# The second MoE's weights: split in place from a DRAM copy, in both arms of a branch, and large chunks with stationary weights

## The chip, the cores and the metric

The kernel runs on one core of a Trainium2 chip. The core has five engines that each work through their own instructions in order: TensorE (PE; its weight loads are listed as PEld), VectorE (DVE), ScalarE (ACT), GpSimd (POOL) and SyncE (SP), which here only starts DMAs. The metric is the device time of one execution in microseconds.

## What is computed

A linear attention gives x (1152 tokens of 512). A first MoE runs all eight experts on every token and weights them by `P`. A second MoE sends each token to one expert; an expert takes the first `capacity` = 288 of its tokens:

```python
# second MoE, x: 1152 x 512, w1: 8 x 512 x 1024, w2: 8 x 1024 x 512
logits = x @ w_gate
expert_idx = np.argmax(logits, axis=1)
probs = softmax(logits)
gate_w = probs[np.arange(N), expert_idx]
# disp[e, place] = x of the token, for the first 288 tokens of each expert
h = np.maximum(disp[e] @ w1[e], 0.0)
y = h @ w2[e]
out[token] = gate_w[token] * y[place]
```

On this input the experts get 2, 9, 314, 22, 1, 2, 779 and 23 tokens.

## The kernel before

Every fp32 product is made of three: a number is split in `hi` (a cast to the narrower format fp32r, on ACT mostly) and `lo` (the number less hi, a subtraction on DVE or POOL), and hi x hi, hi x lo and lo x hi are summed in PSUM.

Attention and the first MoE come first. Their weights come in units (`r` tiles, loaded by SP at L198 and L200), and a scheduler sets the order of their instructions. The second MoE begins near 910 us, and there each engine takes its instructions in the order of the program (`by_hand`).

The second MoE's weights are 64 pieces of 512 KB, eight an expert: pieces 0 to 3 are w1, 4 to 7 are w2. A piece is loaded raw into a 4 KB slot (`load`, L520, tile `rw`); its hi goes to a second slot (`h`, L558), its lo to a third (`l`, L571). The slots are few, and `take` and `done` hand them round. `Splits` deals the work out in halves of 128x512: hi of piece 4 on DVE, the others on ACT, lo of pieces 0, 3 and 5 on POOL, the others on DVE. `sp.rest(nx)` brings the rest of the next expert's splits, but those of pieces 4, 6 and 7 (`LATE`), which come behind the expert's branch.

The loop over the experts handles the first 64 places of each expert (the small chunk) always: `q1_small` (L1103, L1104: 16 matmuls of 512 columns with the tokens' hi and lo stationary), `gt_small` (a copy from PSUM on ACT, L1109), `ht_small` (L1115, transposes), `relu_small` (hi on ACT, L1122; lo on DVE, L1123, the tile `hhl`), `q2_small` (L1130, L1131, 16 matmuls), `out_small` (y on ACT and DVE, L1138, and a scatter on POOL, L1092). The other 224 places, as chunks of 128 and 96, are handled by `large` in an arm that is taken only where a bit of `mask` says that the expert has more than 64 tokens; here these are experts 2 and 6. Both chunks' rows are loaded ahead for every expert (`rows_load`, L1087). In `large` too the tokens are stationary and the weights move: q1 (L1159 to L1162), transposes of h (L1171), q2 (L1182 to L1184).

```python
            with tc.If(mask & (1 << e)):
                large(e, CHUNKS[1:], tails[e], w1, w2)
        sp.need(nx, range(8))
        sp.done(e)
```

Of the kernel before, what the change touches and what calls it, by code (L numbers as in the profile page):

```python
# [20 lines left out]
def tile_linear_attention_two_moe(  # L21
# [125 lines left out]
    # x and its sums (A11, A21 + A22, .. of the seven products), hi and lo, by group and half of the chunks of a block  # L147
# [10 lines left out]
    # the first group's are in slots: the blocks that are made in pairs, and the single ones  # L158
# [31 lines left out]
    class Unit:  # L190
        """an expert's weights for FQ of its features: chunk 2 i + k of W1 is in half k of the rows"""
# [48 lines left out]
    def a_parts(i, key):  # L240
        """the first keys' first columns come by themselves"""
# [18 lines left out]
    def phi_group(hl, g, d, nm):  # L260
        """x w_phi - max|x w_phi| for one or two tiles of rows, both heads of the pair"""
# [101 lines left out]
    def a_xtrans(i, c):  # L363
# [8 lines left out]
        if len(full) < len(TGS[c]):  # L372
            # of a half tile's block, each head's rows have their own columns
# [23 lines left out]
    def x_sums(g, c):  # L397
        """the seven products' left sides; chunk 2 i + k of x is in half k of the columns"""
# [31 lines left out]
    lgs = {}  # L430
    # of each token: its expert, logits, logits less the largest, expert as a number, slot
# [3 lines left out]
    def gate_logits(g):  # L435
        """x w_gate; of the second half S1 = A21 + A22 by the first rows of w_gate, and A22 by what the others are more"""
# [49 lines left out]
    def zero_fill(what):  # L486
        """empty slots and zero rows, from a part of acc that nothing needs yet"""
# [17 lines left out]
    def take(key, shape, dt, name):  # L505
        """the slot that has been free for the longest"""
        at[key] = free.pop(0)
        return slot_at(at[key], shape, dt, name)

    def load(n, keep):  # L510
        """weights of the second layer's experts, in order: n pieces, but leave the slots for hi of keep's"""
        while n and todo:
            e, i = todo[0]
            if len(free) <= sum(x[0] <= keep and x not in sp.h for x in raws) + (e <= keep) + sp.more:
                break
            del todo[0]
            w, cc, W = (w1b, DC // 4, F) if i < 4 else (w2b, F // P // 4, D)
            raws[e, i] = take(("r", e, i), [P, cc, W], F32, f"rw_{e}_{i}")
            r0 = i % 4 * cc * P
            nc.sync.dma_start(raws[e, i], w[e, r0 : r0 + cc * P, :].rearrange("(c p) f -> p c f", p=P))  # L520
            n -= 1

    class Splits:
# [60 lines left out]
        def rest(self, upto):  # L584
            """all that is left of experts upto and before but the late ones of upto, in the order of the weights"""
            while True:
                left = [(q[0][1:], k) for k, q in self.q.items() if q and q[0][1] <= upto]
                left = [x for x in left if not (x[0][0] == upto and x[1] != "p" and x[0][1] in self.LATE)]
                if not left:
                    break  # L590
# [719 lines left out]
```

## Time and profile before

| | |
|---|---|
| median of 3 runs | 1082.06 us (1081.43 to 1083.75) |
| span of the profiled execution | 1079.5 us (its time as a run isn't listed; the median is 2.6 us above the span) |
| busy: PE, DVE, ACT, POOL | 1037.5, 749.9, 401.6, 526.6 us |
| DMA | 95.21 MB, mean 88 GB/s |
| second MoE, 910 us to the end | 169.5 us |

The table of busy times is a mean over stages: PE is busy for 96% of the span, but its idle time lies nearly all in the second MoE.

### The profile page before, as it was taken

To read this page: it belongs to the slowest core of one execution; us is meant where nothing else is said; L and a number is where in the kernel's file an instruction comes from. 1 tells how busy PE (TensorE), PEld (TensorE's weight loads), DVE (VectorE), ACT (ScalarE), POOL (GpSimd) and SP (SyncE) were. 2 spreads that over 40 slices of the span, in tenths; PEclk is the share of its full clock that TensorE was granted. 3 is DMA by queue.
4 is the path that set the end of the run, shared out by engine and by line. 5 is a ranking of instruction groups with operands and counts; after the bars stand their busy time and mean duration, and the time that the engine had idled before them with its cause. 6 is when DMAs were issued, how large, how long until landed. Compare 5 with 4: busy or idle time off the path is not lost. (4 is left out here: it accounts for less than half of the span.)

```text
span 1079.5 us, 16720 instructions
## 1 busy us (share of the span) xinstructions
PE 1037.5 (96%) x6214; PEld 926.3 (86%) x6214; DVE 749.9 (69%) x1400; ACT 401.6 (37%) x841; POOL 526.6 (49%) x524
## 2 busy tenths in 40 slices
PE   7999999999999999999999999999999998798787
PEld 7999989898899899889988988898899888576566
DVE  6755799996666666666666666666667667946962
ACT  5767543322223222222232232223222235717532
POOL 4656897644454554444455544444542016625631
PEclk9999999999999999999999999999999998989889
DMA  8813132211112111111111111111111433967700
GB/s 272 273 53 89 62 98 79 79 59 40 39 40 59 49 51 39 39 40 39 46 53 59 40 40 40 39 41 59 58 57 63 131 110 104 323 229 239 264 7 25
DMA packets 56024, 95.21 MB, mean 88 GB/s; under 512 B 6206, under 2 KB 25022, under 8 KB 55936
## 3 DMA queue, kind: packets, MB, share of 16 engines
q1 hardware_dynamic: 54544, 91.41, 26.4%
q0 software_dynamic: 1392, 2.63, 0.7%
q8 instruction: 55, 0.90, 0.4%
q14 instruction: 33, 0.27, 0.1%
HBM read 84.25 MB, written 11.51 MB: 89 GB/s over the span
## 5 line engine op out<-in xcount | busy, mean ns | idle before, releaser
L81 POOL TENSOR_TENSOR l<-r,h 128x256 fp32r<-128x256 f32 (+2 forms) x100 | 154.2, 1555 | 351.4 <-ACT h L80 351.4
L681 DVE SCALAR_TENSOR_TENSOR acc<-p,prob,acc 128x512 f32<-128x512 f32 x252 | 188.3, 749 | 105.2 <-PE p L672 105.1
L670 PE MATMUL p<-h,hh 128*128 128x512 f32 x576 | 228.4, 396 | 0.0
L671 PE MATMUL p<-l,hh 128*128 128x512 f32 x576 | 227.4, 395 | 0.0
L672 PE MATMUL p<-h,hl 128*128 128x512 f32 x576 | 227.3, 395 | 0.0
L636 DVE TENSOR_TENSOR ca<-ca,p 128x256 f32<-128x256 f32 (+1 forms) x256 | 112.6, 449 | 70.2 <-PE p L619 68.0
L80 ACT CAST h<-r 128x256 fp32r<-128x256 f32 (+2 forms) x108 | 70.9, 686 | 184.8 <-PE p L672 163.6
L625 ACT ACTIVATE hh<-ca 128x320 fp32r<-128x320 f32 (+1 forms) x128 | 56.2, 442 | 217.9 <-DVE ca L636 217.9
L672 PEld LDWEIGHTS p<-h,hl 128*128 128x128 f32 x576 | 108.4, 188 | 25.6
L670 PEld LDWEIGHTS p<-h,hh 128*128 128x128 f32 x576 | 108.4, 188 | 22.4
L671 PEld LDWEIGHTS p<-l,hh 128*128 128x128 f32 x576 | 108.4, 188 | 22.3
L81 POOL TENSOR_TENSOR lt<-t,ht 128x256 fp32r<-128x256 f32 x144 | 124.9, 896 | 1.3 <-PE pn L349 1.3
L571 DVE TENSOR_TENSOR l<-rw,h 128x512 fp32r<-128x512 f32 x80 | 82.8, 1066 | 15.2 <-ACT h L558 13.3
L571 POOL TENSOR_TENSOR l<-rw,h 128x512 fp32r<-128x512 f32 x48 | 69.7, 1474 | 30.1 <-ACT h L558 23.2
L617 PE MATMUL p<-xh,ht 128*128 128x320 f32 x256 | 79.2, 309 | 0.0
L619 PE MATMUL p<-xh,lt 128*128 128x320 f32 x256 | 79.1, 309 | 0.0
L618 PE MATMUL p<-xl,ht 128*128 128x320 f32 x256 | 79.1, 309 | 0.0
L617 PE MATMUL p<-xs,ht 128*128 128x256 f32 x256 | 72.9, 285 | 0.7 <-DVE cb L636 0.5
L619 PE MATMUL p<-xs,lt 128*128 128x256 f32 x256 | 72.6, 284 | 0.0
L618 PE MATMUL p<-xs,ht 128*128 128x256 f32 x256 | 72.4, 283 | 0.0
L636 DVE TENSOR_TENSOR cb<-cb,p 128x320 f32<-128x320 f32 (+1 forms) x128 | 58.0, 453 | 19.0 <-PE p L619 18.0
L629 DVE SCALAR_TENSOR_TENSOR hl<-ca,hh 128x320 fp32r<-128x320 f32 (+1 forms) x128 | 65.7, 515 | 2.5 <-ACT hh L625 2.0
(253 smaller groups left out, 2296.6 us busy)
## 6 DMA issues: line engine op xcount, KB each, us to landing
r<-w1a SPq DMA_DIRECT2D x36, 512.0 KB, 3.5
r<-w2a SPq DMA_DIRECT2D x36, 512.0 KB, 3.8
rw<-w1b SPq DMA_DIRECT2D x32, 512.0 KB, 6.1
rw<-w2b SPq DMA_DIRECT2D x32, 512.0 KB, 8.4
disp<-acc SPq DMA_DIRECT2D x18, 260.0 KB, 4.9
v<-va SPq DMA_DIRECT2D x8, 325.0 KB, 3.7
rawq<-qT SPq DMA_DIRECT2D x8, 320.0 KB, 4.7
out<-acc SPq DMA_DIRECT2D x9, 256.0 KB, 5.5
```

The costliest lines, as they stand in the source:

```text
L80: nc.scalar.copy(hi, src)
L81: (eng or nc.vector).tensor_tensor(lo, src, hi, ALU.subtract)
L571: en.tensor_tensor(self.l[e, i].rearrange("p c f -> p (c f)")[:, ks], rv, hv, ALU.subtract)
L617: nc.tensor.matmul(ps, ws_[0], xs[0], start=i == 0, stop=False)
L618: nc.tensor.matmul(ps, ws_[0], xs[1], start=False, stop=False)
L619: nc.tensor.matmul(ps, ws_[1], xs[0], start=False, stop=i == DI - 1)
L629: nc.vector.scalar_tensor_tensor(lv[:, qs], src, 0.0, hv[:, qs], ALU.max, ALU.subtract)
L636: nc.vector.tensor_tensor(o, x, ps, ALU.add)
L670: nc.tensor.matmul(ps, a, w.w2[0][:, f, :], start=f == 0, stop=False)
L671: nc.tensor.matmul(ps, a, w.w2[1][:, f, :], start=False, stop=False)
L672: nc.tensor.matmul(ps, b_, w.w2[0][:, f, :], start=False, stop=f == FT - 1)
L681: nc.vector.scalar_tensor_tensor(o, ps, prob[:, t, e : e + 1], o, ALU.mult, ALU.add)
```

## The change

While the first MoE runs, `stage` copies the 64 pieces from the weights to a DRAM tensor `wst`, two at each call, in an order in which a piece is contiguous for each partition. The later loads read `wst`. lo is written over the raw piece (`r.bitcast(R32)`), so a piece needs two slots; hi and lo are whole instructions of 128x1024. All hi are on ACT; expert 0's lo on POOL, all others' on DVE. `aside` puts splits of the next two experts into both arms of the branch, in the taken one between the steps of `large`. `large` handles both chunks at once: for each 128 of the 1024 features, the weights are stationary and 224 tokens move (q1), so that h comes out already transposed, and q2 follows per feature block. Rows of the large chunks are loaded in the taken arm. The PSUM pools become 4 and 4 banks, and the scratch for POOL's DMAs is set to 4096 bytes. Comments are dropped.

```diff
+    def stage(n):
+        for e, i in staged[:n]:
+            src = piece(e, i)
+            nc.sync.dma_start(wst[e, i].rearrange("p (c f) -> p c f", c=src.shape[1]), src)
+        del staged[:n]
...
-            nc.sync.dma_start(raws[e, i], w[e, r0 : r0 + cc * P, :].rearrange("(c p) f -> p c f", p=P))
+            nc.sync.dma_start(raws[e, i], wst[e, i].rearrange("p (c f) -> p c f", c=src.shape[1]))
...
-        HI_V, LO_P, LO_P0, LATE = (4,), (0, 3, 5), (1, 2, 5), (4, 6, 7)
...
+                    le = "v" if e else "p"
+                    self.q["a"].append((e, i))
+                    self.q[le].append((e, i))
...
+            h, l = self.h[n], r.bitcast(R32)
+            self.put(eng, lambda: en.tensor_tensor(l, r, h, ALU.subtract))
...
+        def aside(self, hi, lo):
+            steps = {k: [] for k in "avp"}
+            self.put, put = (lambda eng, f: steps[eng].append(f)), self.put
+            self.run("v", -1, lo)
+            self.run("a", -1, hi)
+            self.put = put
+            return steps
...
                 yield from layer2(*pend)
+                stage(2)
...
+        def q1(f):
+            ps = bank2(1, f"q1_{e}_{c0}_{f}")[:, :w]
+            k, fs = f // 4, slice(f * P, (f + 1) * P)
             for c in range(DC):
+                nc.tensor.matmul(ps, w1[0][c][:, fs], xh[:, c], start=c == 0, stop=False)
+                nc.tensor.matmul(ps, w1[0][c][:, fs], xl[:, c], start=False, stop=False)
+                nc.tensor.matmul(ps, w1[1][c][:, fs], xh[:, c], start=False, stop=c == DC - 1)
+            nc.scalar.activation(hh, ps, AF.Relu)
+            nc.vector.scalar_tensor_tensor(hl, ps, 0.0, hh, ALU.max, ALU.subtract)
+            for k in "av":
+                if aside[k]:
+                    aside[k].pop(0)()
...
+        q1(0)
+        for f in range(F // P):
+            if f + 1 < F // P:
+                q1(f + 1)
+            q2(f)
...
         q = q1_small(e, 0, a, w1)
-        sp.run("a", 2, nx)
+        sp.run("v", 8, (e + 1, AHEAD - 1))
...
         hs.append(relu_small(e, 1, ht))
+        sp.run("a", 8, (e + 1, AHEAD + 1))
...
-        sp.rest(nx)
...
+        aside = sp.aside((e + 2, AHEAD + 1), (e + 2, AHEAD - 1))
...
+            with tc.If(mask & (1 << e)) as more:
+                mine = {k: list(x) for k, x in aside.items()}
+                for chunks in SETS:
+                    large(e, chunks, [rows_load(e, c0, n) for c0, n in chunks], w1, w2, mine)
+                for f in mine["a"] + mine["v"]:
+                    f()
+            with more.Else():
+                for f in aside["a"] + aside["v"]:
+                    f()
...
-    nc = bacc.Bacc("TRN2", target_bir_lowering=False, num_devices=1)
+    nc = bacc.Bacc("TRN2", target_bir_lowering=False, num_devices=1, dynamic_dma_scratch_size=4096)
```

DVE before, behind expert 1's branch (`l_2_4` is lo of expert 2's piece 4; L558 is hi, L571 lo, L1123 the `hhl` of expert 2, L1138 the y of expert 1):

```order
L558 CAST h_2_4_10375<-rw_4_9751 128x512
L571 TENSOR_TENSOR l_2_4_10377<-rw_4_9751,h_2_4_10375 128x512
L558 CAST h_2_4_10375<-rw_4_9751 128x512
L571 TENSOR_TENSOR l_2_4_10377<-rw_4_9751,h_2_4_10375 128x512
L571 TENSOR_TENSOR l_2_6_10383<-rw_6_9755,h_2_6_10381 128x512 x2
L571 TENSOR_TENSOR l_2_7_10388<-rw_7_9757,h_2_7_10386 128x512 x2
L1123 SCALAR_TENSOR_TENSOR hhl_0_10442<-ht_0_10437,hhl_0_10442 128x4x64
L1123 SCALAR_TENSOR_TENSOR hhl_1_10452<-ht_1_10447,hhl_1_10452 128x4x64
L1138 SCALAR_TENSOR_TENSOR y_10455<-q_1_10152,tails_9745,y_10455 64x512
L571 TENSOR_TENSOR l_3_1_10481<-rw_1_10073,h_3_1_10433 128x512 x2
L571 TENSOR_TENSOR l_3_2_10484<-rw_2_10075,h_3_2_10445 128x512 x2
```

DVE now, from the start of expert 1's untaken arm on (L567 is lo, written over `rw`; L1105 the `hhl` of expert 2, L1120 the y of expert 1):

```order
L567 TENSOR_TENSOR rw_4_9808<-rw_4_9808,h_2_4_9886 128x1024
L567 TENSOR_TENSOR rw_5_9810<-rw_5_9810,h_2_5_9887 128x1024
L567 TENSOR_TENSOR rw_6_9812<-rw_6_9812,h_2_6_10242 128x1024
L567 TENSOR_TENSOR rw_7_10162<-rw_7_10162,h_2_7_10243 128x1024
L567 TENSOR_TENSOR rw_0_10164<-rw_0_10164,h_3_0_10244 128x1024
L567 TENSOR_TENSOR rw_1_10166<-rw_1_10166,h_3_1_10245 128x1024
L567 TENSOR_TENSOR rw_2_10168<-rw_2_10168,h_3_2_10246 128x1024
L1210 UNCONDITIONAL_BRANCH
L567 TENSOR_TENSOR rw_3_10499<-rw_3_10499,h_3_3_10524 128x1024
L1105 SCALAR_TENSOR_TENSOR hhl_0_10545<-ht_0_10540,hhl_0_10545 128x4x64
L1105 SCALAR_TENSOR_TENSOR hhl_1_10553<-ht_1_10548,hhl_1_10553 128x4x64
L1120 SCALAR_TENSOR_TENSOR y_10560<-q_1_10225,tails_9803,y_10560 64x512
```

Between two experts' `hhl` stood ten halves of lo and two of hi, of the same expert and the next; now eight whole lo stand there, of the next expert and the one behind it, seven of them in the arm.

ACT before, behind expert 3's branch (L558 is hi, L1109 the copy gt of expert 4, L1122 its relu):

```order
L558 CAST h_4_6_11010<-rw_6_10407 128x1024
L558 CAST h_4_7_11015<-rw_7_10409 128x1024
L558 CAST h_5_0_11049<-rw_0_10700 128x1024
L1109 COPY gt_0_11060<-q_4_0_11040 128x512
L558 CAST h_5_1_11062<-rw_1_10702 128x1024
L1109 COPY gt_1_11064<-q_4_1_11051 128x512
L1122 ACTIVATE hhl_0_11071<-ht_0_11066 128x4x64
L558 CAST h_5_2_11074<-rw_2_10704 128x512
```

ACT now, from the start of expert 3's untaken arm on (L559 is hi, L1091 the copies gt of expert 4; hi of `h_4_4` and `h_4_5` and the y of expert 2 stand ahead of the branch, behind expert 3's relus):

```order
L559 CAST h_4_6_10935<-rw_6_10846 128x1024
L559 CAST h_4_7_10936<-rw_7_10848 128x1024
L559 CAST h_5_0_10937<-rw_0_10850 128x1024
L559 CAST h_5_1_10938<-rw_1_10852 128x1024
L559 CAST h_5_2_10939<-rw_2_10854 128x1024
L1210 UNCONDITIONAL_BRANCH
L559 CAST h_5_3_11217<-rw_3_11192 128x1024
L1091 COPY gt_0_11229<-q_4_0_11208 128x512
L1091 COPY gt_1_11231<-q_4_1_11220 128x512
```

Before, casts also stood between the two gt and behind the first relu; now all eight of an expert's period stand between its relus and the next gt.

SP before, among the loads of the first MoE's units 4 to 7 (`r_4` is unit 4's raw weights):

```order
L198 DMA r_4_1827<-w1a 128x4x256
L198 DMA r_5_1990<-w1a 128x4x256
L200 DMA r_4_1829<-w2a 128x2x512
L198 DMA r_6_2130<-w1a 128x4x256
L200 DMA r_5_1992<-w2a 128x2x512
```

and now at the same place (L523 is a copy into `wst`):

```order
L198 DMA r_4_1830<-w1a 128x4x256
L523 DMA wst<-w1b 16x8192
L523 DMA wst<-w2b 256x1x512
L198 DMA r_5_1995<-w1a 128x4x256
L523 DMA wst<-w2b 256x1x512 x3
L523 DMA wst<-w1b 16x8192
L200 DMA r_4_1832<-w2a 128x2x512
L523 DMA wst<-w1b 16x8192 x2
L198 DMA r_6_2137<-w1a 128x4x256
```

About four copies stand between one unit's loads and the next's; all 64 come before the loads of unit 12.

## Rows read from the trace of the kernel before

**Rows 1.** Windows of the second MoE: busy us (instructions) of each engine, clock, DMA.

```profile
930.00:950.00 20.00, 13.87 (x58) 10.74 (x59) 19.42 (x21) 11.30 (x15) 12.82 (x10) 0.79 1.04 346
...
990.00:1010.00 20.00, 12.94 (x53) 10.32 (x53) 19.23 (x18) 11.38 (x15) 14.29 (x11) 0.83 0.81 265
```

**Rows 2.** Waits of PE from 905 us on: total, times, longest.

```profile
PE q L1130 <- DVE hhl L1123: 21.9, 6, 5.4
```

**Rows 3.** Timeline of PE: the first instruction of experts 1 to 6, large arms too.

```profile
921.15 0.47 PE L1103 MATMUL q<-h,xhl 128*128 128x512 f32 x1
...
934.14 0.47 PE L1103 MATMUL q<-h,xhl 128*128 128x512 f32 x1 [0.30 <-PEq L1245]
...
952.51 0.93 PE L1146 MATMUL xst<-ident,xs 128*128 128x128 f32 x8
...
977.77 0.39 PE L1103 MATMUL q<-h,xhl 128*128 128x512 f32 x1
978.00 0.40 PE L1104 MATMUL q<-l,xhl 128*128 128x512 f32 x1
...
988.63 0.47 PE L1103 MATMUL q<-h,xhl 128*128 128x512 f32 x1 [0.30 <-PEq L1245]
...
1007.96 0.47 PE L1103 MATMUL q<-h,xhl 128*128 128x512 f32 x1
...
1022.79 0.47 PE L1103 MATMUL q<-h,xhl 128*128 128x512 f32 x1 [0.30 <-PEq L1245]
...
1038.91 0.93 PE L1146 MATMUL xst<-ident,xs 128*128 128x128 f32 x8
```

**Rows 4.** Timeline of PE: q2's first matmuls after a gap, and matmuls behind one.

```profile
929.82 0.50 PE L1130 MATMUL q<-h,hhl 128*128 128x512 f32 x1 [2.55 <-DVE hhl L1123]
...
945.99 0.79 PE L1130 MATMUL q<-h,hhl 128*128 128x512 f32 x1 [5.45 <-DVE hhl L1123]
...
947.43 0.63 PE L1131 MATMUL q<-l,hhl 128*128 128x512 f32 x1
947.86 0.63 PE L1130 MATMUL q<-h,hhl 128*128 128x512 f32 x1
```

**Rows 5.** Timeline of DVE: lo of a whole slot, and of halves.

```profile
174.07 1.21 DVE L81 TENSOR_TENSOR l<-r,h 128x1024 fp32r<-128x1024 f32 x1
...
939.05 1.65 DVE L571 TENSOR_TENSOR l<-rw,h 128x512 fp32r<-128x512 f32 x1
...
971.19 0.69 DVE L571 TENSOR_TENSOR l<-rw,h 128x512 fp32r<-128x512 f32 x1
```

**Rows 6.** DVE's groups by shape from 905 us on: busy us, mean ns, idle before.

```profile
L571 DVE TENSOR_TENSOR l<-rw,h 128x512 fp32r<-128x512 f32 x76 | 80.1, 1087 | 15.2 <-ACT h L558 13.3
L558 DVE CAST h<-rw 128x512 fp32r<-128x512 f32 x14 | 14.3, 1019 | 1.1 <-DVEq L1245 0.9 <-DMA rw<-w1b 0.2
L1123 DVE SCALAR_TENSOR_TENSOR hhl<-ht,hhl 128x256 fp32r<-128x256 f32 x16 | 6.2, 417 | 3.5 <-ACT hhl L1122 3.5
L1138 DVE SCALAR_TENSOR_TENSOR y<-q,tails,y 64x512 f32<-64x512 f32 x8 | 5.9, 736 | 3.1 <-ACT y L1137 2.8 <-ACTq L1245 0.3
```

**Rows 7.** ACT's groups by shape from 905 us on.

```profile
L558 ACT CAST h<-rw 128x1024 fp32r<-128x1024 f32 x40 | 40.4, 1045 | 11.0 <-issue 6.1 <-POOL l L571 2.3 <-PEq L1245 2.0
L1109 ACT COPY gt<-q 128x512 f32<-128x512 f32 x16 | 9.4, 584 | 9.3 <-PE q L1104 7.1 <-DVEq L1245 1.2 <-DVE h L558 1.1
```

**Rows 8.** Timeline of PE in attention: matmuls of 256 columns.

```profile
20.23 0.28 PE L272 MATMUL pjq<-wbd_h,hlkq 128*128 128x256 f32 x1
20.35 0.22 PE L270 MATMUL pjq<-wbd_h,hhkq 128*128 128x128 f32 x1
```

**Rows 9.** Window of the first MoE: busy us, clock, DMA share, GB/s.

```profile
100.00:150.00 50.00, 49.09 (x369) 44.61 (x368) 38.23 (x70) 27.14 (x70) 44.07 (x49) 1.00 0.27 85
```

**Rows 10.** DMA issues at 124 to 129 us and at 990 to 1010 us: median us to landing.

```profile
r<-w1a SPq DMA_DIRECT2D x1, 512.0 KB, 3.4
...
xs<-disp SPq DMA_DIRECT2D x1, 195.0 KB, 9.0
```

More of the change, by code (lines that the diff above doesn't have):

```diff
@@ L508, in take, with piece @@
         return slot_at(at[key], shape, dt, name)
+    staged = [(e, i) for e in range(E) for i in range(8)]
+    wst = dram.tile([E, 8, P, 4 * P * DC // 2], F32, name="wst")
+    def piece(e, i):
+        w, cc = (w1b, DC // 4) if i < 4 else (w2b, F // P // 4)
+        r0 = i % 4 * cc * P
+        return w[e, r0 : r0 + cc * P, :].rearrange("(c p) f -> p c f", p=P)
+    def stage(n):
[3 more added lines that the diff above has]
+        del staged[:n]
     def load(n, keep):
@@ L513, in load @@
             e, i = todo[0]
-            if len(free) <= sum(x[0] <= keep and x not in sp.h for x in raws) + (e <= keep) + sp.more:
+            if len(free) <= sum(x[0] <= keep and x not in sp.h for x in raws) + (e <= keep):
                 break
             del todo[0]
-            w, cc, W = (w1b, DC // 4, F) if i < 4 else (w2b, F // P // 4, D)
-            raws[e, i] = take(("r", e, i), [P, cc, W], F32, f"rw_{e}_{i}")
-            r0 = i % 4 * cc * P
-            nc.sync.dma_start(raws[e, i], w[e, r0 : r0 + cc * P, :].rearrange("(c p) f -> p c f", p=P))
+            src = piece(e, i)
@@ L533, in __init__ @@
+            self.put = lambda eng, f: f()
             for e in range(E):
                 for i in range(8):
[L535 to L540 removed]
@@ L576, in done @@
         def done(self, e):
-            free.extend(at[k, e, i] for k in "hl" for i in range(8))
+            free.extend(at[k, e, i] for k in "hr" for i in range(8))
         def run(self, eng, n, upto):
-            while n and self.q[eng] and self.q[eng][0][1] <= upto:
-                n -= self.emit(eng, n)
[L584 to L590, printed above, removed]
-                self.emit(min(left)[1])
+            while n and self.q[eng] and self.q[eng][0] <= upto and self.q[eng][0] in raws:
+                self.emit(eng)
+                n -= 1
@@ L822, in moe1_run @@
                         old = [at_ring((w, nx)[j].k, m) for j, m in LAST]
-                        free.extend(old[:12])
+                        free.extend([f"f{n}" for n in range(3)] + old[:12])
                         load(8, -1)
+                        sp.run("p", 6, (0, 7))
                 pend = (u, g, w, h)
@@ L835, in moe1_run @@
         h = yield from layer1(u, 0, w)
-        sp.need(0, range(2))
         free.extend(f"x{n}" for n in range(7))
-        load(7, -1)
+        sp.run("p", 8, (0, 7))
+        load(8, 1)
         yield from layer2(*pend)
@@ L913, in moe1_run @@
         C.turn(2, 2)
+        sp.run("a", 5, (1, 7))
         C.logits(1)
@@ L1062, in tile_linear_attention_two_moe @@
     rings["d"] = ctx.enter_context(pool("ring3", reuse_waits="tile"))
-    free.extend([f"d{n}" for n in range(8)] + ["e0"])
+    free.extend([f"d{n}" for n in range(8)] + ["e0", "e1"])
     tails0 = yp.tile([P, E, RW - D], F32, name="tails0")
@@ L1244, in tile_linear_attention_two_moe @@
                 mask = nc.values_load(many[0:1, 0:1], min_val=0, max_val=(1 << E) - 1)
-            with tc.If(mask & (1 << e)):
-                large(e, CHUNKS[1:], tails[e], w1, w2)
-        sp.need(nx, range(8))
+            with tc.If(mask & (1 << e)) as more:
[7 more added lines that the diff above has]
+                    f()
+        load(8, E)
         sp.done(e)
-        load(4, e + 2)
-        if e + 2 < E:
-            tails[e + 2] = [rows_load(e + 2, c0, n) for c0, n in CHUNKS[1:]]
-        load(8, e + 2)
+        load(4, E)
     out_small(E - 1, done)
```

183 lines of the change are left out of this document (55 added, 128 removed).

## The prediction

> **What bounds the kernel now.** I read the windows of 20 us first, then PE's waits, then PE's row of starts, then DVE and ACT by operation. Up to about 890 us (attention and the first MoE) TensorE is never short of work, and the change gives it nothing there; so the place to look is the last 170 us, the second MoE. There PE is busy 13.9 and 12.9 of 20 us in the two windows shown, while DVE is busy 19.4 and 19.2 [rows 1]. The list of waits names the culprit: q2's first matmul waits 21.9 us in all, six times, for `hhl` of L1123, a DVE instruction [rows 2]. The starts of the experts on PE give the price [rows 3]. Experts 3 and 7 follow the two taken large arms and are quick (977.77 to 988.63: 10.9 us, which is about what PE needs for a small chunk). Five others are gated: expert 1 from 921.15 to 934.14 (13.0), expert 2 to 952.51 (18.4), expert 4 from 988.63 to 1007.96 (19.3), expert 5 to 1022.79 (14.8), expert 6 to 1038.91 (16.1): **81.6 us**. The large arm takes 25.3 us (952.51 to 977.77), and comes twice. After a gap of 2.55 us q2 goes on at once, after one of 5.45 us its matmuls start 0.43 us apart [rows 4] instead of 0.23 (977.77 to 978.00 [rows 3]): the clock has fallen to its lower level, and the gap is paid a second time.
>
> Why is `hhl` late? DVE works in order, and ahead of it stand the weight splits of this expert's pieces 4, 6, 7 and, one expert earlier, 1 and 2: ten halves of lo and two halves of hi for each expert. A half of lo takes 0.69 us when POOL is quiet (971.19) and 1.65 us when POOL splits too (939.05) [rows 5]; the means are 1.087 and 1.019 us [rows 6]. With two hhl (0.417) and one y (0.736), DVE needs 10 x 1.087 + 2 x 1.019 + 2 x 0.417 + 0.736 = **14.5 us** for an expert. That is the gated period.
>
> **The change, part by part.** *DVE alone.* Now it takes all eight lo, whole: 1.21 us for 128x1024 at 174.07 us, where POOL didn't work beside it [rows 5]. POOL's part is gone after expert 0, DVE's casts too: 8 x 1.21 + 0.834 + 0.736 = **11.3 us** an expert, and 0.3 as a mean for xhl, which comes every second expert.
>
> *ACT alone for hi.* Eight casts of 1.045, two gt of 0.584 [rows 7], two relus and one y (for these I take DVE's 0.417 and 0.736 for the same tiles): 11.1 us, and ACT can't cast while it waits for q1 or ht. The order puts all eight casts between the relus of one expert and gt of the next, so gt waits for them: some 8.4 us, of which q2 and the next q1 on PE cover about 8. This loop of about 11 us with 1 to 2 us of handing over is the one that I expect to set the period, with DVE close behind.
>
> *Loads.* Eight pieces of 0.52 MB are 4.2 MB an expert. At the 346 GB/s of the window 930 to 950 [rows 1] that is 12.1 us. This would be the bound if each expert had to be fetched in its own period. It has not: 41 pieces are left for the loop, 41 x 1.5 = 62 us of the 135 us that it lasts, and the large arms, when DMA has nothing else, take their share. A piece now needs two slots instead of up to three, so loads go further ahead.
>
> So a gated period is at best 11.3 (DVE or ACT without any handing over) and at worst as now. I walked the three queues through expert by expert with these durations and got 12.9, 12.2, 14.9, 11.9 and 13.8 for experts 1, 2, 4, 5 and 6: **65.7 us, or 15.9 less**. (Five times 11.3 would be 56.5, a gain of 25.1; nothing gained would be 81.6.) Experts 0, 3 and 7 I leave as they are.
>
> *Both arms split.* In the taken arm one cast and one lo stand behind each relu and `hl`. Per f, ACT then has 0.4 + 1.05 and DVE 0.4 + 1.21, against PE's 2.5 us or more: hidden. If a cast in the arm waited for its load, relu behind it on ACT, and with it PE, would wait too; the order shows only pieces there that were asked for a whole expert earlier.
>
> *The large arm.* Per arm: eight transposes as now, 0.93; 96 matmuls of 224 columns; 48 of 512 columns at 0.23 = 11.2. 256 columns start 0.12 us apart (20.23 and 20.35 [rows 8]); by columns 224 are 0.105, and 0.12 is the upper end, so I take 0.113: 10.8 us. The sixteen transposes of h fall away. To the 22.9 come about 1.1 for the first x split and for the last f, whose relu and `hl` nothing covers: **24.0 instead of 25.3, 2.5 less for both** (2.5 is the value for 0.113; 0.12 makes it 1.1, 0.105 makes it 4).
>
> *Rows in the arm.* Two loads now start only when SP has reached the branch. SP gets there an expert early, when it isn't held by a slot: I take nothing. If it comes as late as PE, the price is at most a load behind others, 9.0 us for such rows [rows 10], in each arm.
>
> *The copies.* 64 DRAM to DRAM copies stand on SP's queue among the first twelve units' r loads. No such copy is in the trace. Bounds: a piece's 1.5 us at 346 GB/s, or twice that, since it is read and written: 97 to 194 us of DMA. The stretch of some 190 us in which they run has its DMA engines busy for 0.27 [rows 9], so 139 us are free. An r load landed 3.4 us after its issue [rows 10] and POOL then has its sums to make before PE needs the unit, so a copy or two ahead of it is no loss: I take nothing, with the upper end (194 - 139 = 55 us of DMA work too many, some of which the later units absorb) kept for the rival.
>
> *Scratch of 4096.* It could make the scatters on POOL follow each other more slowly. Nothing that the first two experts need hangs on the last of them, and of the outputs only the last scatter matters: nothing.
>
> **Sum** against the profiled span: 1079.5 - 15.9 - 2.5 + 1.5 (one gap of about 3 us will still bring the clock down for part of a q2: half of 16 matmuls, 0.2 us more each) = 1062.6. The median of the runs is 2.6 above the span, and I leave that: **1065 us**, 17 less.
>
> **A rule against it.** The new large loop cycles through two PSUM banks, q1 to relu to `hl` to q2, where the old one had matmuls in runs of 24. In the trace, gaps up to 2.55 us cost no clock [rows 4], and the new loop's waits should be under 0.5 us, so by the rows the arm stays at the upper level. The Trainium skill, "TensorE: Matmul & The Clock Gate" (A second HAM failure mode: psum-queue depth-cycling), says that short idle times between groups of matmuls which cycle through PSUM banks can be enough to make the clock swing between its levels. By that rule the arm would lose instead of gain; it is rival 3, priced there from rows.
>
> **The rivals.** 1. *Less gain* (22%). ACT's eight casts in a row hold gt, DVE waits for them, and each gated period stays at about 15 us: 75 instead of 81.6, with the arms 1082.06 - 6.6 - 2.5 = 1073. For it: DVE's lo already waits 13.3 us for ACT's casts [rows 6], and ACT gets the 14 half casts that DVE does now. Against it: of DVE's 14.5 us, 3 are gone.
> 2. *More gain* (8%). Everything is ready, and the gated experts come at 10.9 as expert 3 does: 54.5, a gain of 27.1, with the arms 1052.
> 3. *The clock falls in the large arm* (6%), the slower side. Its 22 us of matmuls would take 0.43/0.23 as long: 41, 19 more in each arm, 38 for both: 1103. It decides (17 us) as soon as the lower level holds for 45% of the arms. Against it: no wait there that I can find is longer than 0.5 us.
> 4. *Copies hold up the first MoE* (5%), slower too. With 2.4 us and more for a copy, r loads come later than POOL's slack allows, and PE, never idle there now, waits: 17 to 40 us more, so 1083 to 1105.
> 5. *No change* (5%). The loads bound each expert at 12.1 and a wait for a slot comes on top, so the periods stay: 1082.
>
> **How the numbers follow.** The first case, my forecast, has 54%, and its own range is 1058 to 1070 (terms of 1 to 4 us for each of two arms, and 2 us for a period or two). The range of 1054 to 1078 takes in all of that, nearly all of rival 1 and some of rival 2, about 8 in 10. About 0.2% (2 us) is what a measurement of this kernel can tell from no change. Faster: my forecast and rivals 1 and 2, 84%. Same: 5%. Slower: 11%.
>
> **What would show it.** In the new profile, DVE's lo should be near 1.2 us, with no POOL split beside it after expert 0. PE's wait for `hhl` should fall from 21.9 to under 12 us, and what is left may be put down to gt (ACT). The large arm should take 23 to 25 us at full clock, with 224 columns at 0.105 to 0.12. PE should stay fully busy between 100 and 250 us, and unit starts there move by under 1 us. I am wrong if DMA landings, not DVE or ACT, end the waits of q1 and q2; if the clock in the large arm shows its lower level; or if the span up to 890 us grows.

## The result and the profile after

The changed kernel takes **1056.6 us** (median of 4 runs, 1053.85 to 1059.04) where the one before, run beside it, takes 1081.74: a ratio of 0.9767, 95% interval 0.9736 to 0.9798, or 25 us less. The profiled execution has a span of 1055.9 us (1057.68 as a run), against 1079.5.

The stretch that the prediction was read from comes first. These are the windows of 20 us of the changed kernel (busy us of PE, PEld, DVE, ACT, POOL with their instructions, granted clock, DMA share, GB/s), the same stretch as in [rows 1]:

```profile
930.00:950.00 20.00, 17.67 (x99) 14.75 (x98) 11.91 (x16) 10.84 (x18) 7.95 (x2) 0.91 0.99 368
950.00:970.00 20.00, 20.00 (x123) 17.04 (x121) 9.07 (x12) 7.68 (x13) 1.92 (x2) 1.00 0.08 26
970.00:990.00 20.00, 16.09 (x78) 12.96 (x77) 15.31 (x18) 17.51 (x24) 11.86 (x2) 0.91 0.91 351
990.00:1010.00 20.00, 16.82 (x88) 13.24 (x86) 17.57 (x18) 15.76 (x22) 15.79 (x2) 0.97 0.67 250
```

PE is now the busiest engine in two of the four, at 17.67 and 20.00 of 20 us; DVE, which filled the windows before with over 19, is at 9 to 18, and the clock stands at 0.91 and more instead of 0.79 and 0.83. The large arm (most of 950 to 970) runs at the full clock with hardly a load. What PE still waits for in the second MoE (total, times, longest; compare [rows 2]):

```profile
PE q L1112 <- DVE hhl L1105: 5.3, 3, 1.8
PE ht L1097 <- ACT gt L1091: 3.8, 3, 1.7
```

`hhl` is down from 21.9 to 5.3 us, and beside it the wait for `gt`, a copy on ACT, has grown from 0.3 us to 3.8. And these are PE's starts of the experts from 0 to 7, large arms too (those lines that begin with an xst transpose), the counterpart of [rows 3]:

```profile
907.54 0.47 PE L1085 MATMUL q<-h,xhl 128*128 128x512 f32 x1
...
917.41 0.47 PE L1085 MATMUL q<-h,xhl 128*128 128x512 f32 x1
...
929.03 0.47 PE L1085 MATMUL q<-h,xhl 128*128 128x512 f32 x1 [0.30 <-PEq L1210]
...
941.99 0.38 PE L1132 MATMUL xst<-ident,xs 128*128 128x128 f32 x2
...
965.70 0.39 PE L1085 MATMUL q<-h,xhl 128*128 128x512 f32 x1
...
976.01 0.47 PE L1085 MATMUL q<-h,xhl 128*128 128x512 f32 x1 [0.30 <-DVE y L1120]
...
990.89 0.47 PE L1085 MATMUL q<-h,xhl 128*128 128x512 f32 x1
...
1001.29 0.47 PE L1085 MATMUL q<-h,xhl 128*128 128x512 f32 x1 [0.30 <-DVE y L1120]
...
1016.82 0.38 PE L1132 MATMUL xst<-ident,xs 128*128 128x128 f32 x2
...
1040.53 0.39 PE L1085 MATMUL q<-h,xhl 128*128 128x512 f32 x1
```

Differences of such starts give the ledger (in the kernel before, expert 0 starts at 910.67 us and expert 7 at 1064.11). "Gated five" are the small chunks of experts 1, 2, 4, 5 and 6. "Routing" is the time from the start of the first MoE's last matmul to that of the loop's first; in it the tokens are dealt out to their experts:

| us | before | after | less |
|---|---|---|---|
| gated five | 13.0 + 18.4 + 19.3 + 14.8 + 16.1 = 81.6 | 11.6 + 13.0 + 14.9 + 10.4 + 15.5 = 65.4 | 16.2 |
| routing | 16.7 | 10.0 | 6.8 |
| two large arms | 25.3 + 25.2 | 23.7 + 23.7 | 3.0 |
| experts 0, 3, 7 and the tail | 36.7 | 35.5 | 1.2 |
| up to the first MoE's last matmul | 893.9 | 897.6 | -3.6 |
| span | 1079.5 | 1055.9 | 23.6 |

Two lines of it I had not forecast: the 6.8 us of the routing, and the 3.6 us that the part before it lost.

**The routing.** First the kernel before: the last matmuls of the first MoE end at 894.3 us; then PE has to wait for a one-hot row `oh` on DVE (L735). DVE, POOL and PE there:

```profile
892.73 3.23 DVE L735 TENSOR_TENSOR oh<-iota_e,rt_e 128x16 bf16<-128x16 f32 x1
...
892.42 0.97 POOL L785 DMA_INDIRECT disp<-acc,slot_i  x1 [0.31 <-issue]
893.40 2.51 POOL L571 TENSOR_TENSOR l<-rw,h 128x512 fp32r<-128x512 f32 x2
...
896.01 0.17 PE L750 MATMUL cp<-oh,tri_b 128*128 128x8 bf16 x1 [1.69 <-DVE oh L735]
```

A comparison of 16 numbers a partition lasts 3.23 us, until POOL's two splits are through (893.40 + 2.51 = 895.91). PE stands still for 1.69 and soon after 0.9 us, and then the clock drops: the next window has PE busy all the time at a granted clock of 0.50, the lower level.

```profile
900.00:905.00 5.00, 5.00 (x24) 5.00 (x25) 2.50 (x14) 4.33 (x6) 3.90 (x4) 0.50 0.12 41
```

In the changed kernel POOL has no splits there. The same instruction, and a window of its routing stretch (897.6 to 907.5):

```profile
896.35 0.18 DVE L727 TENSOR_TENSOR oh<-iota_e,rt_e 128x16 bf16<-128x16 f32 x1
```

```profile
898.00:903.00 5.00, 5.00 (x52) 4.99 (x51) 4.10 (x25) 3.46 (x6) 0.86 (x1) 1.00 0.64 188
```

It takes 0.18 us, PE doesn't wait for it, and the clock is full. (The two windows don't hold the same instructions, so their counts don't compare; the 16.7 and 10.0 us of the whole stretch do.) A scatter of POOL ran beside this `oh` too (896.06 us, 0.97), so it is the split, not the scatter, that held it. By the Trainium skill, "SBUF — State Buffer" (SBUF: two separate sides), a DVE instruction with two SBUF inputs and a POOL instruction that reads SBUF exclude each other for a whole instruction. The end of `oh` agrees with that: it comes at 895.96 us, just behind the splits' 895.91. Its start doesn't settle it: as the trace has it, `oh` starts 0.67 us ahead of the splits.

### The profile page after: what moved, and what is told of

It reads as the page before. It is cut to its first block, busy times and chain, and to the rows that moved or that the text cites. A ratio compares the mean times of both kernels' runs of the same rounds, so it can differ in the third digit from the quotient of the medians.

```text
span 1055.9 us, 16779 instructions
## 1 busy us (share of the span) xinstructions
PE 1028.5 (97%) x6278; PEld 923.9 (87%) x6278; DVE 721.9 (68%) x1370; ACT 404.2 (38%) x840; POOL 509.8 (48%) x484
## 5 line engine op out<-in xcount | busy, mean ns | idle before, releaser
L621 DVE SCALAR_TENSOR_TENSOR hl<-ca,hh 128x320 fp32r<-128x320 f32 (+1 forms) x128 | 69.5, 544 | 2.3 <-ACT hh L617 1.6
L628 DVE TENSOR_TENSOR cb<-cb,p 128x320 f32<-128x320 f32 (+1 forms) x128 | 57.9, 453 | 18.8 <-PE p L611 17.7
L567 DVE TENSOR_TENSOR rw<-rw,h 128x1024 fp32r<-128x1024 f32 x56 | 65.0, 1212 | 4.3 <-ACT h L559 3.7
L559 ACT CAST h<-rw 128x1024 fp32r<-128x1024 f32 x64 | 62.9, 1046 | 7.1 <-PE p L663 4.5
```

The source lines that it names most:

```text
L567: self.put(eng, lambda: en.tensor_tensor(l, r, h, ALU.subtract))
L621: nc.vector.scalar_tensor_tensor(lv[:, qs], src, 0.0, hv[:, qs], ALU.max, ALU.subtract)
L628: nc.vector.tensor_tensor(o, x, ps, ALU.add)
```

## The experiments

Ratios are to the kernel before, with 95% intervals; all diffs are against the changed kernel. The kernels of the first part ran on one chip and those of the second on another; in the third, fewer_slots and casts_3 shared a chip, and the two w2_late kernels shared another. Stage times are those of one profiled execution each.

### What the prediction took for free, and the stretches it did not look at

**few_copies**: only expert 0's eight copies to DRAM are made, and all experts load these, so experts 1 to 7 compute with expert 0's weights; the amount of work stays.

```diff
         for e, i in staged[:n]:
+            if e:
+                break
...
-            nc.sync.dma_start(raws[e, i], wst[e, i].rearrange("p (c f) -> p c f", c=src.shape[1]))
+            nc.sync.dma_start(raws[e, i], wst[0, i].rearrange("p (c f) -> p c f", c=src.shape[1]))
```

> The changed kernel, with copies of expert 0's eight pieces alone; all experts load these eight (so experts 1 to 7 compute with expert 0's weights; the amount of work in the second MoE is the same). Theory: the 56 other copies cost nothing but the waits for prob (1.9 us in the changed kernel) in the first MoE: last matmul of the first MoE 0 to 1.5 us earlier against its start, ratio to before 0.975 to 0.978. Rival, the copies cost the whole 3.6 us by which that matmul came later than before: ratio 0.973. Rival 4 of the prediction (17 us and more) would give 0.96.

Measured: 1054.37 us, 0.9739 (0.9708 to 0.9769). The first MoE, from its first to its last matmul of layer 2, takes 766.75 us with these eight copies alone, 768.3 and 767.5 in two executions with them, and 766.9 in the kernel before. The window that answers to [rows 9], of the changed kernel and of this one:

```profile
100.00:150.00 50.00, 49.82 (x380) 45.92 (x380) 36.11 (x68) 28.40 (x75) 42.23 (x47) 1.00 0.73 248
```

```profile
100.00:150.00 50.00, 49.11 (x369) 44.64 (x369) 38.06 (x69) 27.32 (x71) 44.10 (x49) 1.00 0.28 85
```

The copies raise the DMA share from 0.28 to 0.73, and PE is as busy there as without them. Behind this window PE waits 1.9 us in all for `prob`, a tile that DVE writes, where the traces of this run and of the kernel before list no such wait; in the other eleven executions with all 64 copies that wait is 0 to 1.1 us. The first MoE takes 765.5 to 768.3 us in these twelve, so by these rows the copies cost under 2 us, which doesn't stand out from the spread.

Of the 3.6 us lost before the routing, 2.3 aren't the copies': they arise before layer 2's first matmul, which comes at 129.3 us in the changed kernel, at 126.0 in its second execution (below), at 127.2 in this run and at 127.0 in the kernel before. The clock accounts for them: it falls in attention, where no copy is issued yet (none in the first 30 us), to 0.56 in this window of the changed kernel, where the kernel before has 1.00:

```profile
15.00:20.00 5.00, 5.00 (x28) 5.00 (x28) 3.76 (x9) 2.79 (x6) 2.69 (x4) 0.56 0.32 84
```

Of the twelve other executions of the changed kernel and its variants only that of fewer_slots shows this fall.

**pool_late**: expert 0's last split on POOL, and its cast on ACT with it, is held back until after the first tokens' routing has begun, so that it stands where the kernel before had its splits.

```diff
-        sp.run("p", 8, (0, 7))
+        sp.run("p", 8, (0, 6))
...
         B.turn(1)
+        sp.run("p", 1, (0, 7))
```

> The changed kernel, with one lo of expert 0 (piece 7, on POOL) and its cast put back into the routing, behind POOL's first four scatters. Theory: a POOL split there holds up small DVE operations on which PE waits (before, oh of L735 took 3.23 us instead of 0.18), and the gap takes the clock down: from the last matmul of the first MoE to the first of the loop 14 to 17 us instead of 10.4, clock below 0.9 there, ratio 0.980 to 0.983. Rival: the stretch became short because DVE's and ACT's own splits left it; one POOL split costs under 1 us, ratio 0.977.

Measured: 1059.84 us, 0.9804 (0.977 to 0.9838). One instruction on POOL brings the whole stall back; DVE and POOL, PE's waits, and the window after them:

```profile
889.88 3.11 DVE L727 TENSOR_TENSOR oh<-iota_e,rt_e 128x16 bf16<-128x16 f32 x1
...
890.56 2.39 POOL L567 TENSOR_TENSOR rw<-rw,h 128x1024 fp32r<-128x1024 f32 x1
```

```profile
PE cp L742 <- DVE oh L727: 1.6, 1, 1.6
PE x2t L705 <- DVE acc L673: 0.9, 1, 0.9
```

```profile
895.00:900.00 5.00, 4.78 (x23) 4.78 (x24) 3.20 (x21) 3.57 (x6) 1.97 (x2) 0.50 0.96 351
```

Routing takes 16.60 us here and 16.74 before. Without a split of POOL in it, it takes 9.98 in the changed kernel's profile, 11.30 in its second one and 11.62 in few_copies beside this run. So one split there costs 5.0 to 6.6 us, and that it is the cause is shown by rows. Between 9.98 and 11.62 lies a fall of the clock that some executions without a split have as well; this is few_copies, where PE has no wait listed from 880 to 900 us:

```profile
895.00:900.00 5.00, 5.00 (x35) 5.00 (x36) 3.48 (x24) 4.07 (x6) 0.97 (x1) 0.74 0.62 193
```

By the median, pool_late is 5.5 us above few_copies and 3.2 above the changed kernel's first one. Not all of a stage's loss reaches the end: experts 1 and 2 take 13.22 + 9.78 = 23.0 here instead of 24.6 us.

**tokens_still**: the large arm as it was (tokens stationary, h transposed), with the splits between its steps.

```diff
-                nc.tensor.matmul(ps, w1[0][c][:, fs], xh[:, c], start=c == 0, stop=False)
...
+                nc.tensor.matmul(ps, xx_[i][0][:, c], w1[0][c][:, fs], start=c == 0, stop=False)
...
+                nc.tensor.transpose(ps[:, c * P : c * P + n], gts[i][f][:n, c * P : (c + 1) * P], ident[:n, :n])
```

> The changed kernel, with the large arm of before (tokens stationary, h transposed), the splits beside it kept. Theory: PE's work alone, 25.2 instead of 23.7 us for each arm, 3.1 us in all: ratio 0.979 to 0.980. Rival: the arms' form also decides whether the splits fit beside them, and more comes back: over 6 us, ratio above 0.982.

Measured: 1057.35 us, 0.977 (0.9741 to 0.9799), 3.0 us above few_copies beside it and 0.8 above the changed kernel's first median; the intervals don't part it from either. By rows the arms take 25.06 and 24.98 us instead of 23.71 each, so the stationary weights are worth 2.6 us of the 25.

**prebranch**: the splits between the steps of `large` run ahead of the branch instead.

```diff
         aside = sp.aside((e + 2, AHEAD + 1), (e + 2, AHEAD - 1))
+        for f in aside["a"] + aside["v"]:
+            f()
+        aside = {k: [] for k in "avp"}
```

> The changed kernel, with the splits of both arms put ahead of the branch, so that the taken arm has to wait for them. Theory: ACT's five casts (5.2 us) and DVE's seven lo (8.5 us) end 4 to 5 us behind q2, and x's split of the taken arm waits for that, so each of the two arms begins 4 to 5 us later, with the clock down behind the gap; experts without the arm as now: ratio 0.985 to 0.987. Rival: the splits are needed in any case and are only moved, so what the arm loses the next expert gets back: within 2 us, ratio 0.977 to 0.979.

Measured: 1063.66 us, 0.9827 (0.9793 to 0.986), 9 us slower than few_copies beside it. Its largest part has one place, expert 2's arm (30.08 instead of 23.71 us). Expert 6 has only four splits left there; they end at 1023.3 us, just before the arm begins (1023.46), and it stays at 23.72. The gated five take 68.1 us. DVE and PE in it:

```profile
936.62 8.02 DVE L567 TENSOR_TENSOR rw<-rw,h 128x1024 fp32r<-128x1024 f32 x7
944.57 1.14 DVE L81 TENSOR_TENSOR xl<-xst,xh 128x448 fp32r<-128x448 f32 x2
```

```profile
945.23 0.56 PE L1144 MATMUL q<-xl,h 128*128 128x224 f32 x1 [3.47 <-DVE xl L81]
945.59 0.41 PE L1145 MATMUL q<-xh,rw 128*128 128x224 f32 x1
945.80 0.41 PE L1143 MATMUL q<-xh,h 128*128 128x224 f32 x1
```

Seven splits in a row stand ahead of the tokens' own, and PE waits 3.47 us and then works more slowly. Placing one split behind each step, as the change does, avoids 6.4 us here.

### ACT's casts in a row, and DVE against DVE and POOL

**after_again** is the changed kernel once more, beside the next three.

> The changed kernel itself once more, beside the others of this group: 0.977 as before, within 0.002. Its profile shows how far one execution's stages move by themselves: both theories expect the first MoE within 1.5 us and expert 4 within 1.5 us.

Measured: 1055.17 us, 0.9761 (0.9742 to 0.978). Gated five 65.7 us, arms 23.71 each, routing 11.30.

**casts_gt**: in the changed kernel the eight casts between one expert's relus and the next gt stand two ahead of y (`out_small`) and six behind it, five of these in the arm. Here the two go elsewhere, one behind the first gt and one behind the first relu; six in a row are left.

```diff
         gts = [gt_small(e, 0, q_)]
+        sp.run("a", 1, (e + 1, AHEAD + 1))
...
         hs = [relu_small(e, 0, ht)]
+        sp.run("a", 1, (e + 1, AHEAD + 1))
...
-        sp.run("a", 8, (e + 1, AHEAD + 1))
...
-        aside = sp.aside((e + 2, AHEAD + 1), (e + 2, AHEAD - 1))
+        aside = sp.aside((e + 2, AHEAD - 1), (e + 2, AHEAD - 1))
```

> The changed kernel, with two of the eight casts of an expert's period moved: one behind the first gt, one behind the first relu, so that six are left between the relus and gt. Theory (ACT's casts in a row hold gt, xhl and y, and with them DVE and PE): PE's wait for gt falls from 3.8 us to under 1, experts 4 and 6 lose 2 to 3 us each of their 15, expert 1 about 1: 4 to 8 us, ratio 0.970 to 0.973. Rival (DVE's eight lo set the period): gt comes earlier, the wait moves to hhl and the sum of the five gated periods stays within 1.5 us of 65.4: ratio 0.976 to 0.978.

Measured: **1047.19 us**, 0.9699 (0.968 to 0.9718). Gated five 59.3 instead of 65.7; PE's waits in the second MoE:

```profile
PE q L1112 <- DVE hhl L1105: 3.5, 4, 1.2
...
PE ht L1097 <- ACT gt L1091: 0.6, 2, 0.3
```

The wait for gt is gone, and the clock of the whole span is 0.996 instead of 0.989. The casts in a row did hold gt; but gt isn't what ends last ahead of q2. DVE and PE in expert 4 of the changed kernel, whose eight splits lie between the first two lines (975.90 to 985.05, shown in the last section), and DVE in that of casts_gt:

```profile
975.23 0.74 DVE L1120 SCALAR_TENSOR_TENSOR y<-q,tails,y 64x512 f32<-64x512 f32 x1
...
984.98 0.74 DVE L1105 SCALAR_TENSOR_TENSOR hhl<-ht,hhl 128x256 fp32r<-128x256 f32 x2
...
985.44 0.80 PE L1112 MATMUL q<-h,hhl 128*128 128x512 f32 x1 [1.77 <-DVE hhl L1105]
```

```profile
969.17 9.15 DVE L567 TENSOR_TENSOR rw<-rw,h 128x1024 fp32r<-128x1024 f32 x8
978.26 0.74 DVE L1105 SCALAR_TENSOR_TENSOR hhl<-ht,hhl 128x256 fp32r<-128x256 f32 x2
```

In both, `hhl` stands right behind DVE's eight splits, and these begin right behind y. In the changed kernel y, and the tokens' split ahead of it, wait for ACT, where the two casts stand ahead of their counterparts. So the eight splits begin only 0.1 us ahead of the expert's first matmul (976.01) there, and 1.6 ahead (970.80) in casts_gt. In experts 2 and 6 too, `hhl` stands right behind the eight. Part of the gain is the clock: in expert 6 it is 1.00 instead of 0.77, and the expert takes 11.7 instead of 14.7 us.

**casts_y**: only the place ahead of y is cleared: the two casts go behind `out_small`, and all eight stand in one row ahead of gt.

```diff
-        sp.run("a", 8, (e + 1, AHEAD + 1))
...
             out_small(e - 1, done)
+        sp.run("a", 8, (e + 1, AHEAD + 1))
```

> The changed kernel, with the two casts that stand ahead of xhl's cast and y on ACT put behind them (in the same iteration). Theory (DVE starts its eight lo late because y and xhl stand ahead of them in its order, and these wait for ACT's two casts): DVE's lo begin 1.3 to 2 us earlier in experts 4 and 6, about as much less in their periods: ratio 0.973 to 0.975. Rival (lo waits for its own hi anyway, which now comes 1.3 us later): no change, 0.977.

Measured: 1049.98 us, 0.9718 (0.9693 to 0.9743); gated five 60.6. This has 5.1 of the 6.4 us that casts_gt gains in the gated five, though PE still waits 3.0 us for gt. What is freed here is y, and with it the start of DVE's splits (1.2 us ahead of expert 4's first matmul). So the larger part goes by y and not by gt; what freeing gt alone would bring no run shows.

**lo_shared**: lo of pieces 0, 3 and 5 of each expert goes to POOL again, all else as changed (the lines that put POOL's splits into the arms are left out here).

```diff
-                    le = "v" if e else "p"
+                    le = "v" if e and i not in (0, 3, 5) else "p"
...
+        sp.run("p", 8, (e + 1, AHEAD - 1))
...
```

> The changed kernel, with lo of pieces 0, 3 and 5 of experts 1 to 7 on POOL again (whole, in place), DVE's other five as now. Theory (the two engines block each other): DVE's 128x1024 rises from 1.21 to 1.8 us or more, POOL's takes 2.5 to 3.2, so that DVE needs 5 x 1.8 + 1.6 = 10.6 us instead of 11.3 for an expert and POOL's late pieces hold q1: the gated periods gain nothing, ratio 0.977 to 0.983. Rival (DVE's own time is what counts, and it falls): DVE's lo stays near 1.3 us and the gated periods fall by 2 us each, ratio 0.968 to 0.972.

Measured: 1057.39 us, 0.9783 (0.9768 to 0.9799), gated five 17.2 + 9.6 + 14.8 + 17.4 + 9.5 = 68.4. The groups of lo in the second MoE (busy us, mean ns, idle before), first of the changed kernel, then of this one:

```profile
L567 DVE TENSOR_TENSOR rw<-rw,h 128x1024 fp32r<-128x1024 f32 x56 | 65.0, 1212 | 4.3 <-ACT h L559 3.7 <-DMA xs<-disp 0.6
```

```profile
L567 POOL TENSOR_TENSOR rw<-rw,h 128x1024 fp32r<-128x1024 f32 x21 | 55.2, 2655 | 5.4 <-ACT h L559 5.3
L567 DVE TENSOR_TENSOR rw<-rw,h 128x1024 fp32r<-128x1024 f32 x35 | 55.1, 1619 | 1.8 <-ACT h L559 1.1 <-DMA xs<-disp 0.6
```

With 21 of 56 splits taken off it, DVE is busy for 55.1 instead of 65.0 us: each of those left takes 1.62 instead of 1.21. But the time lost is 3.0 us by the sum of the gated five (2.7 against after_again beside it), which is far less than the 16.2 that they had gained. So DVE alone isn't the whole of the gain, and the next part asks for the rest.

### What is worth what

**fewer_slots**: 4 slots instead of 10 are handed to the second MoE at its start.

```diff
-    free.extend([f"d{n}" for n in range(8)] + ["e0", "e1"])
+    free.extend([f"d{n}" for n in range(4)])
```

> The changed kernel with 34 instead of 40 slots for the second MoE's weights (d4 to d7, e0 and e1 left out), so that fewer pieces are there ahead: between two hhl DVE now has the four lo of the next w2 and the four of the w1 behind it, whose loads are asked for later. Theory (how far the loads run ahead is a condition of the gain: with fewer slots each expert's pieces are fetched in its own period, 10 to 12 us for eight, and lo waits for landings): the five gated periods rise from 65.4 to 72 to 80 us, ratio 0.983 to 0.990. Rival (40 slots are more than needed, DVE's and ACT's times alone count): within 2 us, ratio 0.976 to 0.979.

Measured: 1058.2 us, 0.9778 (0.9759 to 0.9796), which the intervals don't part from after_again. Gated five 65.8; experts 0 and 3 take 1.3 and 1.2 us more.

**casts_3**: as casts_gt, but with places for a cast behind each gt and behind the first relu, and the arm's limit lower, for lo too. The expectation speaks of two casts moved and none behind the relu; so it comes out in experts 4 and 5, where no cast is left for the third place.

```diff
         gts = [gt_small(e, 0, q_)]
+        sp.run("a", 1, (e + 1, AHEAD + 1))
...
         gts.append(gt_small(e, 1, q))
+        sp.run("a", 1, (e + 1, AHEAD + 1))
...
         hs = [relu_small(e, 0, ht)]
+        sp.run("a", 1, (e + 1, AHEAD + 1))
...
-        sp.run("a", 8, (e + 1, AHEAD + 1))
...
-        aside = sp.aside((e + 2, AHEAD + 1), (e + 2, AHEAD - 1))
+        aside = sp.aside((e + 2, AHEAD - 2), (e + 2, AHEAD - 2))
```

> As the kernel with two casts moved behind the first gt and the first relu (ratio 0.970), but one behind the first gt and one behind the second gt, none behind the relu. Theory (ACT has idle time between gt and relu, and either place serves; DVE's 11.5 us an expert are the bound by now): 0.969 to 0.971. Rival (a cast between gt and relu delays relu by up to 1 us, and with it hhl and q2): expert periods 0.5 us longer each, 0.972 to 0.974.

Measured: **1045.96 us, 0.9671** (0.9654 to 0.9689), the lowest median of the study, though the intervals don't part it from casts_gt. Gated five 11.1 + 11.8 + 12.9 + 10.6 + 11.6 = 57.9; gt is waited for 0.3 us, `hhl` 4.3 in six short waits. The first arm takes 24.52; PE waits for the tokens' rows twice, 1.5 us in all.

**w2_late**: an order nearer to that of before, in which an expert's w2 is split only behind its own q1, and the next w1 only at the branch; DVE alone as changed.

```diff
-        sp.run("v", 8, (e + 1, AHEAD - 1))
+        sp.run("v", 8, (e, 7))
...
-        sp.run("a", 8, (e + 1, AHEAD + 1))
+        sp.run("a", 8, (e + 1, 1))
...
-        aside = sp.aside((e + 2, AHEAD + 1), (e + 2, AHEAD - 1))
+        aside = sp.aside((e + 1, 5), (e + 1, 3))
```

> The changed kernel with half an expert less of splits ahead, as the kernel before had it: in the arms only the next expert's w1 is split, and an expert's own w2 behind its branch, right ahead of its hhl on DVE and of its gt on ACT. DVE alone does lo. Theory A (how far ahead the splits stand is what shortened the gated periods): they rise from 65.4 to 73 us or more, and experts 3 and 7, which profit from splits in the large arm, become 3 us longer each: ratio 0.985 to 0.993. Theory B (the two engines' mutual blocking was the loss, and DVE alone is the gain): 65 to 68 us, ratio 0.976 to 0.980.

Measured: 1053.88 us, 0.9748 (0.9728 to 0.9767). Gated five 63.7, so nothing is lost. PE now waits 6.0 us for DVE's lo inside q1, but in 15 waits of at most 0.6, and the clock stands at 1.00 in four of the five.

**w2_late_shared**: that order, and pieces 0, 3 and 5 on POOL as in lo_shared.

```diff
-                    le = "v" if e else "p"
+                    le = "v" if e and i not in (0, 3, 5) else "p"
...
-        sp.run("v", 8, (e + 1, AHEAD - 1))
+        sp.run("v", 8, (e, 7))
+        sp.run("p", 8, (e, 7))
...
```

> The same, and lo of pieces 0, 3 and 5 on POOL again as well. With the changed kernel, the one with shared lo (0.978) and the one with late w2 this makes a square. Theory A: as the late order with DVE alone, plus 2 to 3 us: 0.987 to 0.996. Theory B: the loss of sharing shows fully only where nothing is ahead: gated periods near the 81.6 us of before, ratio 0.992 to 1.0, while late order with DVE alone stays below 0.980. Rival C (neither; it was the casts on DVE, the halves and the slots): below 0.983.

Measured: 1070.03 us, 0.9895 (0.9873 to 0.9916). Gated five 11.4 + 17.1 + 18.1 + 17.9 + 17.7 = 82.1, about the 81.6 of before, though by another wait. Its groups of lo and the longest of PE's waits in the second MoE:

```profile
L567 DVE TENSOR_TENSOR rw<-rw,h 128x1024 fp32r<-128x1024 f32 x35 | 63.5, 1856 | 6.8 <-ACT y L1169 4.1 <-ACT h L559 2.1 <-DVE hhl L1106 0.6
L567 POOL TENSOR_TENSOR rw<-rw,h 128x1024 fp32r<-128x1024 f32 x21 | 60.1, 2880 | 6.1 <-ACT h L559 6.0
```

```profile
PE q L1087 <- POOL rw L567: 20.3, 8, 5.2
```

PE waits here for POOL's own lo inside q1, and no longer for `hhl` at q2, as it did for 21.9 us in the kernel before.

Four kernels make a square of the gated five:

| us | splits an expert ahead | w2 split late |
|---|---|---|
| lo on DVE alone | 65.4 (after) | 63.7 (w2_late) |
| lo on DVE and POOL | 68.4 (lo_shared) | 82.1 (w2_late_shared) |

With w2 split late, DVE alone is worth 18.4 us; with the splits ahead it is worth 3.0. The order is worth 13.7 when POOL shares the work and nothing (-1.7) when it doesn't. The medians have the same order (ratios 0.977, 0.975, 0.978 and 0.990). Either cure is enough, and their gains don't add. What the square shows is the price of sharing and late order together; that the kernel before lost its time by the same wait as w2_late_shared it doesn't show.

## Why the prediction was right, and where it was off

The forecast was 1065 us, with a range of its own of 1058 to 1070 inside the wide one of 1054 to 1078; 1056.6 came. The mechanism in the second MoE is borne out in the main, and one term outside it was missed.

**The bound.** Right: DVE's queue was the gate, and once lo was one instruction on one engine its mean fell to 1.212 us (1.21 in [rows 5] had been taken). That sharing makes DVE's work longer the last experiments show too: 35 lo beside POOL's 21 keep DVE busy for 63.5 us, nearly as long as all 56 do alone. But PE's 20.3 us of waiting there are for POOL's lo, so that run is no second proof of the queue.

**The gated experts.** 65.7 was forecast and 65.4 came: 12.9, 12.2, 14.9, 11.9 and 13.8 against 11.6, 13.0, 14.9, 10.4 and 15.5. The sum is better than its parts, which are off by up to 1.7 and cancel; that is luck. That ACT's eight casts, by holding gt, would set the pace with DVE close behind is half right. The casts cost 6 us (casts_gt), but mostly by holding y and so the start of DVE's eight splits, and in experts 2, 4 and 6 `hhl` behind these splits is what PE waits for last. The 75 us of rival 1 did not come, but ACT's row of casts was the largest part of what was left to gain: casts_3 ends at 57.9, not far from the 54.5 of rival 2.

**Loads.** That two slots a piece let loads go further ahead was one of my reasons. fewer_slots takes six slots away and leaves the gated five at 65.8, so the number of slots handed over at the start isn't it; beyond that the point stays open, since the loads were not otherwise changed.

**The large arm.** 24.0 was forecast, 23.7 measured, 3.0 us less for both instead of 2.5 (0.3 of the 0.5 is arithmetic: 48 x 0.23 is 11.0 and not 11.2, in each arm). The 224 columns start 0.11 us apart, as PE's timeline in the arm shows:

```profile
948.02 0.28 PE L1144 MATMUL q<-xl,h 128*128 128x224 f32 x1
948.13 0.27 PE L1145 MATMUL q<-xh,rw 128*128 128x224 f32 x1
```

0.113 had been taken. The clock is 1.00 over 950 to 970, so rival 3 did not come. By the rule of the Trainium skill, "TensorE: Matmul & The Clock Gate" (A second HAM failure mode: psum-queue depth-cycling), it could have; the trace doesn't show it here.

**Copies, rows in the arm.** Taking the copies at nothing was right within 2 us. The rows asked for in the arm made PE wait 1.5 us in casts_3 and 0.2 in casts_gt, and in no other of these runs. Unit starts move by more than the 1 us that I allowed, 2 to 4 us, and the stretch up to 890 us, whose growth was to be a sign of being wrong, grew by 3.6. That sign was badly chosen: in the second execution the first MoE's last matmul comes at 893.5 us, with 893.9 before, and the larger part of the 3.6 is the clock in attention. The scratch no run tests.

**The clock.** I had put one drop at 1.5 us on top, so 67.2 with the gated five. Three drops came, in experts 2, 4 and 6 (granted clock 0.87, 0.89 and 0.78), and are inside the 65.4. The premise that gaps up to 2.55 us cost no clock was wrong in the trace of before already: in its routing the clock falls behind gaps of 1.69 and 0.9 us.

**The step that was mis-sized** is that up to the loop the change "gives it nothing there". The routing stretch gave 6.8 us. The sum had the span 16.9 less, and it became 23.6 less; the difference is as large as that term because the others, 3.5 more (gated five, arms, experts 0, 3 and 7) and 3.6 less (the part before), happen to cancel. In the second execution the routing gave 5.4 and the part before lost nothing. POOL's splits and DVE's `oh` stood in the trace of before. The prediction was read from windows up to 250 us and from 910 us on, and not from the 17 us ahead of the loop. The time lies within the wide range only because 1054 allowed for rival 2, whose mechanism (every gated expert as quick as expert 3) did not come; that, too, is luck.

## What to carry to other kernels

When one kind of work is shared between DVE and POOL, compare the mean duration of an instruction with and without the other engine at work, since the busy time may show as load what is mutual waiting; then cure either the sharing or the order, and don't count both gains. Work that is moved ahead of a dependent chain is placed one instruction at a time between the links of the chain (gt, relu, y), not as a block ahead of them; and it is asked which queue that block holds up next, as ACT's casts held DVE's splits by way of y. And a change that takes work off an engine is looked for in every stretch where that engine was busy, the short ones between the stages first.

## What the runs showed of the hardware that was not expected

A long run of DVE instructions held POOL's DMA. DVE and POOL in expert 4 of the changed kernel:

```profile
975.90 9.15 DVE L567 TENSOR_TENSOR rw<-rw,h 128x1024 fp32r<-128x1024 f32 x8
...
976.25 9.59 POOL L1074 DMA_INDIRECT out<-y,tails  x1 [7.87 <-DVE y L1120]
...
1013.01 0.91 POOL L1074 DMA_INDIRECT out<-y,tails  x1 [1.90 <-DVE y L1120]
```

The scatter of 64 rows that takes 0.91 us at 1013.01 takes 9.59 beside eight splits, and ends (985.84) just after the last of them (985.05). It isn't released between two of the eight. It happens to four of the eight scatters and costs nothing here, as nothing waits for those rows.

The length of a gap alone does not decide on the clock. In the kernel before, a gap of 2.55 us left the full clock [rows 4]; in the changed one a gap of 1.76 us was followed by the lower level:

```profile
936.63 0.50 PE L1112 MATMUL q<-h,hhl 128*128 128x512 f32 x1 [1.76 <-DVE hhl L1105]
936.96 0.41 PE L1113 MATMUL q<-rw,hhl 128*128 128x512 f32 x1
937.19 0.60 PE L1112 MATMUL q<-h,hhl 128*128 128x512 f32 x1
937.59 0.63 PE L1113 MATMUL q<-rw,hhl 128*128 128x512 f32 x1
```

The second matmul comes 0.33 us and the third 0.23 after the one ahead, and from there on they are 0.40 to 0.43 apart for 3.4 us. In experts 4 and 6 the first matmul behind a gap of 1.77 us runs at the lower level already; there a gap of 1.75 and of 1.09 us stood shortly ahead. And in the routing of few_copies the clock fell with PE busy all the time. What else decides, these runs don't show.
